# Hashed attention, a Mish feed-forward and eight experts on one core: who decodes the feed-forward weights, when they are converted, and how attention's planner prices transfers

## The chip, the cores and the metric

One core of a Trainium2 chip. The metric is the device time of one execution in microseconds, the median of several runs. Engines are named as in the profile: PE is TensorE's matmul, PEld its weight load, DVE is VectorE, ACT is ScalarE, POOL is GpSimd, SP is the engine that issues the DMA transfers.

## The reference

```
attention:  B,H,S,D = 2,8,768,64;  bits = (q @ proj > 0), six per query and per key
            mask = equal buckets;  attn = softmax(where(mask, q k^T / 8, -1e9));  x = attn @ v
            -> x of 1536 tokens x 512
feed-forward:  h = x @ w_in (512 x 2048, float64 weights);  g = h * tanh(softplus(h));  x = g @ w_out
experts:  logits = x @ w_gate;  P = exp(logits - max), 8 rounds of row and column scaling
          out = sum over 8 experts of P[:, e] * (relu(x @ w1[e]) @ w2[e])      (512 x 1024 x 512 each)
```

The feed-forward weights arrive as 64-bit floats; everything else is float32.

## The kernel before

Three parts follow each other in one instruction stream: attention, the feed-forward, the experts. Every large product is done with operands split into a rounded high part and a low remainder (fp32r), three matmuls per tile: high x high, high x low, low x high.

**Feed-forward.** The hidden width 2048 is cut into 16 chunks of 128; a chunk's weights (its slice of both matrices) are one [128, 1024] array of 64-bit numbers. A step is one chunk for one block of 512 tokens, 48 steps in all: chunks go in groups of 2, 2, 4, 4 and 4, and for each group the three token blocks follow. In step n TensorE does `up(n)` (lines 790 to 801, 12 matmuls: lines 798 and 799 read the weight's high part, line 800 its low part) and `down(n - 3)` (lines 813 to 826, 12 matmuls into four accumulators). In between, `act(n)` (lines 803 to 811) applies Mish and a rounding on ACT and a subtraction on DVE (line 810). At the end of a group the four accumulators are evacuated: the first group by ACT (line 831), the others by DVE (line 833).

**Decoding.** A chunk comes in two halves, each loaded by one 512 KB transfer (line 131) into one of three stage buffers. `decode` turns a half into float32 in eight parts: parts 0 and 1 scale the high and low words on ACT (lines 148 and 150); part 2 clamps (152), part 3 shifts (154), part 4 merges the sign (156), part 5 masks the exponent (160), all on DVE; part 6 multiplies the low word by the power of two, on POOL (162); part 7 adds high and low on DVE or POOL (164) and, in the feed-forward, issues the load of the half three places on. Then `convert_hi` (line 176, ACT) rounds a whole chunk into its place in a ring of eight, and `convert_lo` (line 182, POOL) subtracts to get the low part.

**The order in the feed-forward** is written out by the loop at lines 1059 to 1080. Each engine takes its instructions in that order. A half's parts 0 to 3 come right after the step's `up`, parts 4 to 6 at the end of the step (key d + 0.5), part 7 at the end of the next (d + 1.4). Lines 1042 to 1057 lay the halves out, one every 1.15 steps from step 0, and put the two conversions of a chunk at the end of step t (`at(t, ...)`), t at least two after the step of its second half. Functions registered for n - 1.5 run at the very beginning of step n, before `up(n)`. Chunks 0 and 1 are decoded inside attention.

**Attention.** 16 heads, two units of 384 queries each. Its order is made by a planner when the kernel is built (lines 484 to 751): every piece of work is a task with an engine, a cost, a due time (plus an offset per kind from `OFF`) and the tasks it waits for. The planner takes, per engine, the task with the least "earliest start + DELTA x due", and emits it. For transfers (engine "Q", issued by SP) lines 727 to 730 say when the data counts as landed:

```
free[e] = start + (cost or 0.6)
bus = max(free[e] + 0.5, bus) + lag
ends[k] = bus + RECEIPT
```

Transfers in attention are loads of queries and keys (line 264), of values (270), of the 64-bit weights (131), and copies within the chip (335): six moves of 192 KB for each head, four of bits (18 KB) and one row per unit. `DUE0` and `PACE` set when the four half chunks 0 to 3 are decoded beside attention; their part 6 is a task of engine "P", part 7 of "D" or "P". Three more half chunks are loaded ahead for the feed-forward.

**Experts.** 64 units, lines 1085 to 1284, products of a seven-multiplication scheme (line 1119) and the second product (1186). Nothing in it is touched.

Of the kernel before, what the change touches and what calls it, by code (L numbers as in the profile page):

```python
# [16 lines left out]
P = 128  # L17
# [20 lines left out]
NS = 4  # L38
# [13 lines left out]
COLD = 7.5  # L52
FILL = 256
AHEAD = (1, 2)
OFF = {'weight_lo': 11.0, 'add': -10.2, 'weight_load': -52.8, 'norm6': 87.2, 'prep_hi': 3.9, 'norm_move': -73.0, 'load_qk': -0.2, 'norm0': -29.7, 'load_v': -23.9, 'decode': -0.3, 'bits_mm': 4.8, 'norm1': -110.3, 'norm5': -85.1, 'st_exp': -3.3, 'norm7': 55.1, 'rows_cp': -157.2, 'av_mm': -0.1, 'rows_move': -39.6, 'rows_mm': 3.5, 'norm4': -106.6, 'norm3': 12.6, 'sum_mm': -2.3, 'bits_cmp': -16.6, 'av_one': 12.2, 'weight_hi': 293.4, 's_max': 6.6, 'st_mm': 2.5, 'prep_move': -6.4, 'prep_lo': -4.7, 'bits_move': -9.7, 's_mm': 2.4}
DELTA = 0.0374
RECEIPT = 1.6
DIRECT = 4
DUE0 = 52
PACE = 38  # L60
NX = 1
NATT = 2
FG = 4
# [4 lines left out]
Q = 32  # L68


def f32(t):
    return t[:].bitcast(F32)
# [3 lines left out]
def lsh_attention_moe_kernel(  # L76
# [13 lines left out]
    nc = tc.nc  # L90
# [21 lines left out]
    sgn = [dec_p.tile([P, 512], I32, name=f"sgn{i}") for i in range(2)]  # L112
# [31 lines left out]
    def decode(i, j, part, e="P"):  # L144
        t = staged[i, j]
        lw, hw = t[:, :, 0], t[:, :, 1]
        if part == 0:
            nc.scalar.activation(f32(hw), f32(hw), AF.Copy, scale=SCALE64)
        elif part == 1:
            nc.scalar.activation(f32(lw), lw.bitcast(U32), AF.Copy, scale=2.0 ** -52)  # L150
        elif part == 2:
            nc.vector.tensor_scalar(out=f32(hw), in0=f32(hw), scalar1=HIGH64, scalar2=-HIGH64, op0=ALU.min, op1=ALU.max)
        elif part == 3:
            nc.vector.tensor_scalar(out=sgn[j], in0=hw, scalar1=3, scalar2=None, op0=ALU.logical_shift_left)
        elif part == 4:
            nc.vector.scalar_tensor_tensor(
                out=hw, in0=hw, scalar=-0x80000000, in1=sgn[j], op0=ALU.bitwise_and, op1=ALU.bitwise_or
            )
        elif part == 5:
            nc.vector.tensor_scalar(out=sgn[j], in0=hw, scalar1=-0x800000, scalar2=None, op0=ALU.bitwise_and)  # L160
        elif part == 6:
            nc.gpsimd.tensor_mul(f32(lw), f32(lw), f32(sgn[j]))  # L162
        else:
            (nc.gpsimd if e == "P" else nc.vector).tensor_add(
                dec[i % NDEC][:, j * 512:(j + 1) * 512], f32(hw), f32(lw)
            )
            staged.pop((i, j))
            if auto[0]:
                load_next()
# [18 lines left out]
    def attention():  # L188
        with ExitStack() as a:
# [294 lines left out]
            tasks, ends = {}, {}  # L484

            def task(engines, due, f, *args, after=(), cost=None, lag=0.01, ring=None, frees=None):
                due += OFF.get(f.__name__ + (str(args[1]) if f is norm else ""), 0)
                tasks[f.__name__, *args] = (engines, cost, due, f, args, list(dict.fromkeys(after)), lag, ring, frees)
# [8 lines left out]
                    bits_cmp=0.47, clear=0.7, clear_start=0.85, proj_parts=0.7, gate_parts=0.45,  # L497
# [8 lines left out]
            SEEN = {"E": 0.28, "A": 0.05, "D": 0.05, "P": 0.06}  # L506
            HELD = 0.13
            PICK = (prep_lo, add, norm, decode)
            MOVE = dict(lag=0.87)
            nm = lambda f, *args: (f.__name__, *args)  # L510

            def st_done(u):
                return [nm(st_mm, u, c) for c in range(NKC)] if u >= 0 else []
# [21 lines left out]
            for i in range(NS):  # L535
                for n, kind in enumerate(("sq", "bk", "one")):
                    e = "D" if (kind, i) in FAST else "P"
                    task(e, -8.5 + 3 * i + n / 4, clear, kind, i, after=[nm(clear, "bk", i)] * (n == 2) + [nm(hold)] * (i > 0))

            for h in range(NH):  # L540
                due = 6 * (uses(h)[0] - 3)
                old = uses(h - NS)[1] if h >= NS else -1
                shared = [h for h in range(NH) if h not in (1, 2, *AHEAD)]
                hin = shared[shared.index(h) - NRAW] if h in shared and shared.index(h) >= NRAW else None
                single = [x for x in range(NH) if x not in AHEAD]
                prior = single[single.index(h) - 1] if h and h not in AHEAD else None
                moved = [nm(prep_move, prior, j) for j in range(6)] if prior is not None else []
                task("Q", due - 24 if h else -99, load_qk, h, lag=1.75 if h else -0.35, cost=0.6 if h else 1.2,
                     after=[nm(bits_mm, hin)] + [nm(prep_lo, hin, i) for i in range(2)] if hin is not None else [])
                his = [nm(prep_hi, h, i) for i in range(len(halves(h)))]  # L550
                los = [nm(prep_lo, h, i) for i in range(2)]
                for i in range(len(halves(h))):
                    task("A", due - 14.0 if h else -50, prep_hi, h, i, cost=None if h else 0.45,
                         after=[nm(load_qk, h), *moved])
                for i in range(2):
                    task("PD" if h else "D", due - 14.0 + 1 if h else -50, prep_lo, h, i, after=[his[i if h == 0 else 0], *moved] + [los[0]] * i)
                task("E", due - 10.0 if h else -50, bits_mm, h, cost=None if h else 1.1, after=[nm(load_qk, h), nm(proj_parts)] + [nm(bits_move, h - 2, x) for x in range(4) if h > 2], ring="r" if h else None, frees=nm(bits_cmp, h))
                if h:
                    task("D", due - 9.0, bits_cmp, h, after=[nm(bits_mm, h)] + [nm(bits_move, h - 2, x) for x in range(4) if h > 2])
                else:  # L560
                    for i, j in ((0, 0), (0, 1), (1, 1), (1, 0)):
                        task("D", due - 9.0 + i + 18 * (i > j), bits_cmp, 0, i, j, cost=0.6, after=[nm(bits_mm, 0), nm(load_const, 1), nm(clear, ("sq", "bk")[j], 0)])
                for j in range(6):
                    engine, kw = ("A", {}) if h < 3 and j < 2 else ("Q", MOVE)
                    task(engine, due - 5.0 + 0.1 * j, prep_move, h, j, after=(his if j < 4 else los) + st_done(old), **kw)
                for x in range(4 if h else 0):
                    task("Q", due - 5.0 + 0.5 + x / 8, bits_move, h, x, lag=0.3, cost=0.7,
                         after=[nm(bits_cmp, h), nm(clear, "sq", h % NS), nm(clear, "bk", h % NS)] + st_done(old))

                freed = [av_done(u, NKC // AVG - 1) for x in (h // 2 * 2 - 4, h // 2 * 2 - 3) for u in uses(x)] if h > 3 else []  # L570
                task("Q", 24 * (h // 2) - 20.0, load_v, h, after=freed + [nm(prep_move, 0, j) for j in range(2, 6)] * (h < 2) + [nm(prep_move, 1, j) for j in range(6)] * (1 < h < 4), lag=1.4)
# [3 lines left out]
            for u in range(NU):  # L575
# [9 lines left out]
                ready = [nm(rows_cp, u)]  # L585
                if not direct:
                    ready = [nm(rows_move, u)]
                    task("Q", due + 6.5, rows_move, u, after=[nm(rows_cp, u)] + st_done(u - 2 * NS), lag=0.01)
                ready += [nm(prep_move, h, j) for j in range(6)] + [nm(clear, "one", h % NS)]
                for c in range(NKC):  # L590
                    i = 6 * u + c
# [117 lines left out]
            while count < len(tasks):  # L709
# [16 lines left out]
                    keep_warm(int(max(0.0, real - free[e] - 0.25) / (0.21 if real < COLD else 0.12)))  # L726
                if e == "Q":
                    free[e] = start + (cost or 0.6)
                    bus = max(free[e] + 0.5, bus) + lag
                    ends[k] = bus + RECEIPT  # L730
                else:
                    if cost is None:
                        cost = COST[e][f.__name__]
                    end = real + cost
                    if e == "P" or e == "D" and shares(k):
                        held[e] = end - (0.05 if e == "D" else 0.0)
                    free[e] = end - OVER[e]
                    ends[k] = end + SEEN[e]
# [180 lines left out]
    def at(n, f, *args):  # L919
        side.setdefault(n, []).append(lambda: f(*args))  # L920
# [109 lines left out]
    free = {}  # L1030
# [11 lines left out]
    for i in range(RING_A, N64):  # L1042
        need = free[i - RING] + 1 if i >= RING else 0
        if NATT <= i:
            nd = max(nd, free_dec.get(i - NDEC, 0))
            for j in range(2):
                d = int(nd)
                for part, lag in enumerate((0, 0, 0, 0, 0.5, 0.5, 0.5, 1.4)):
                    early.setdefault(d + lag, []).append((i, j, part, "D"))
                nd += 1.15  # L1050
            need = max(need, d + 2)
        nxt = max(nxt, need)
        t = nxt
        at(t, convert_hi)
        at(t, convert_lo)
        free_dec[i] = nxt + 1
        nxt += 1

# [275 lines left out]
```

## Time and profile before

| | |
|---|---|
| median of 3 runs | 1506.09 us (1505.69 to 1508.87) |
| profiled execution | 1504.85 us, span 1503.1 us, mean granted clock 0.995 |
| PE busy | 1478.4 us, 98% of the span |
| DVE, ACT, POOL busy | 872.1, 638.3 and 910.0 us |
| chain that ended last | PE 94%, DVE 3%, all others 1% or less |
| HBM read | 93.41 MB, 64 GB/s over the span |

Busy times are sums over the whole span; the three parts have different limits, so what matters is read from stretches of it. The chain is followed back from the last instruction to whatever released each one. A wait of an engine is named by the line that waited and the line that released it. PEclk is the share of TensorE's full clock that was granted, as a mean over the stretch.

### The profile page before, as it was taken

How to read it: one execution, taken by the hardware profiler on the slowest of the kernel's cores; microseconds unless marked ns; L12 is line 12 of the kernel's file. 1: busy time of each engine (PE TensorE's matmuls, PEld its weight loads, DVE VectorE, ACT ScalarE, POOL GpSimd, SP SyncE). 2: the span in 40 equal slices, each digit the busy share in tenths (PEclk: the TensorE clock that was granted, in tenths of full speed). 3: DMA queues.
4: the chain of work that ended last, by engine and by line, in shares of the span. 5: the costliest groups of instructions: out<-in, count | busy, mean ns of one | idle time of the engine just before them, and what ended most of it. 6: DMA issues, size and time to landing. Idle time of an engine off the chain costs nothing.

```text
span 1503.1 us, 20188 instructions
## 1 busy us (share of the span) xinstructions
PE 1478.4 (98%) x7452; PEld 1260.5 (84%) x7452; DVE 872.1 (58%) x1406; ACT 638.3 (42%) x1161; POOL 910.0 (61%) x762
## 2 busy tenths in 40 slices
PE   9999999989999999999999999999999999999998
PEld 6666667768887899989899998989989899998987
DVE  7878868858725566665445477653534535344353
ACT  5655666534434343434334333343433334333331
POOL 7778874324322776666666666666666666666660
PEclk9999999999999999999999999999999999999999
DMA  7655512212200122222122222232222122222211
GB/s 190 175 150 156 153 36 98 71 56 84 84 1 15 47 80 70 71 70 71 60 67 70 71 70 71 65 104 70 71 70 70 65 64 69 71 71 71 69 44 42
DMA packets 66490, 116.70 MB, mean 78 GB/s; under 512 B 18276, under 2 KB 20440, under 8 KB 66392
## 3 DMA queue, kind: packets, MB, share of 16 engines
q1 hardware_dynamic: 66392, 115.43, 25.3%
q8 instruction: 58, 0.95, 0.3%
q14 instruction: 40, 0.33, 0.1%
HBM read 93.41 MB, written 3.15 MB: 64 GB/s over the span
## 4 chain that ended last, share of the span: by engine, by line
PE 94%; DVE 3%; DMA 1%; ACT 1%; issue 1%; POOL 1%; SPq 0%; DVEq 0%; POOLq 0%; ACTq 0%
PE y L1186 35%; PE u L1119 31%; PE y L823 7%; PE pav L442 4%; PE h L800 3%; PE h L798 2%; PE h L799 2%; PE pst L414 2%; PE ps L379 2%; PE pst L415 2%; PE psum L452 1%; PE pbits L353 1%; POOL w L182 0%; DMA sb<-hi 0%; DVE mx L384 0%
## 5 line engine op out<-in xcount | busy, mean ns | idle before, releaser
L1127 ACT ACTIVATE gh<-c 128x384 fp32r<-128x384 f32 x256 | 134.6, 526 | 174.2 <-DVE c L1139 172.1
L1139 DVE TENSOR_TENSOR u<-u,p 128x384 f32<-128x384 f32 x64 | 35.7, 558 | 283.8 <-PE u L1119 283.8
L1132 DVE SCALAR_TENSOR_TENSOR gl<-c,gh 128x384 fp32r<-128x384 f32 x256 | 196.0, 829 | 0.0
L1186 PE MATMUL y<-ww,gh 128*128 128x512 f32 x768 | 186.6, 391 | 0.0
L1186 PE MATMUL y<-w,gh 128*128 128x512 f32 x768 | 186.0, 391 | 0.0
L1186 PEld LDWEIGHTS y<-w,gh 128*128 128x128 f32 x768 | 143.7, 188 | 28.9
L1186 PEld LDWEIGHTS y<-ww,gh 128*128 128x128 f32 x768 | 143.7, 188 | 28.8
L1003 POOL TENSOR_TENSOR w<-stage,w 128x1024 fp32r<-128x1024 f32 x32 | 76.5, 2390 | 89.1 <-ACT w L999 89.1
L1003 POOL TENSOR_TENSOR ww<-stage,ww 128x1024 fp32r<-128x1024 f32 x32 | 76.5, 2390 | 81.7 <-ACT ww L999 81.7
L162 POOL TENSOR_TENSOR stage<-stage,sgn 128x512 f32<-128x512 f32 x32 | 42.1, 1317 | 116.2 <-DVE sgn L160 91.6
L823 PE MATMUL y<-gh,w 128*128 128x512 f32 x336 | 110.0, 390 | 0.0
L999 ACT CAST ww<-stage 128x1024 fp32r<-128x1024 f32 x32 | 33.6, 1049 | 157.5 <-PE y L1186 157.5
L979 POOL TENSOR_TENSOR wa<-stage,wa 128x512 fp32r<-128x512 f32 x32 | 45.5, 1423 | 89.2 <-ACT wa L974 80.1
L999 ACT CAST w<-stage 128x1024 fp32r<-128x1024 f32 x32 | 33.6, 1049 | 154.5 <-PE y L1186 154.5
L1186 PE MATMUL y<-ww,gl 128*128 128x512 f32 x384 | 98.2, 389 | 0.0
L1186 PE MATMUL y<-w,gl 128*128 128x512 f32 x384 | 97.7, 389 | 0.2 <-DVE gl L1132 0.2
L979 POOL TENSOR_TENSOR wx<-stage,wx 128x512 fp32r<-128x512 f32 x32 | 45.3, 1417 | 80.7 <-ACT wx L974 80.7
L384 DVE TENSOR_REDUCE mx<-ps 128x1 f32<-128x768 f32 x96 | 88.0, 949 | 9.9 <-PE ps L379 8.5
L420 ACT ACTIVATE p<-pst 128x384 f32<-128x384 f32 x162 | 71.4, 490 | 51.3 <-PE pst L415 44.2
L1119 PE MATMUL u<-tw,w 128*128 128x384 f32 x480 | 91.7, 336 | 0.0
L1119 PE MATMUL u<-tw,ws 128*128 128x384 f32 x480 | 91.6, 336 | 0.0
L810 DVE TENSOR_TENSOR gl<-t,gh 128x512 fp32r<-128x512 f32 x48 | 48.6, 1012 | 64.9 <-ACT gh L809 62.5
(206 smaller groups left out, 3706.9 us busy)
## 6 DMA issues: line engine op xcount, KB each, us to landing
stage<-in_w_dram SPq DMA_DIRECT2D x160, 512.0 KB
raw<-in_qk_dram SPq DMA_DIRECT2D x13, 384.0 KB
sb<-hi SPq DMA_DIRECT2D x20, 192.0 KB
vt<-in_v_dram SPq DMA_DIRECT2D x16, 192.0 KB
out_dram<-acc SPq DMA_DIRECT2D x11, 256.0 KB
wx<-hi SPq DMA_DIRECT2D x14, 192.0 KB
zq<-hi SPq DMA_DIRECT2D x10, 192.0 KB
ak<-hi SPq DMA_DIRECT2D x10, 192.0 KB
```

The lines of the kernel that those rows point to most:

```text
L384: nc.vector.tensor_reduce(out=mx_t[u % 2][:, t:t + 1], in_=s_t.pop((u, t))[:, :, :HALF], axis=AX.XY, op=ALU.max, negate=True)
L420: nc.scalar.activation(p_t[u, c][:, :HALF], st_t.pop((u, c))[:, :HALF], AF.Exp, scale=0.125)
L442: nc.tensor.matmul(av_t[n][64 * e:64 * e + 64, :WIDE], vt[head(u) // 2 % 2][:, c, e, :], p_t[u, c][:, :WIDE], start=(c == 0), stop=(c == N ...
L810: nc.vector.tensor_sub(lo, a, f32(hi))
L823: nc.tensor.matmul(yps[j], x, y, start=(head and m == 0), stop=(tail and m == 2))
L979: nc.gpsimd.tensor_sub(a[:, 1, 0:512], t[:, 0, :], f32(a)[:, 0, 0:512])
L999: nc.scalar.copy(wbuf[u % 2]["w"][:, 0, :], staged["u", u, 1].rearrange("p c n -> p (c n)"))
L1003: nc.gpsimd.tensor_sub(y[:, 1, :], t, f32(y)[:, 0, :])
L1119: nc.tensor.matmul(bank[x], weight(u, a, m, kc), moving(u, b, mm, kc), start=(first and n == 0), stop=(n == 5), skip_group_check=not first)
L1127: nc.scalar.activation(hi, src, AF.Relu)
L1132: nc.vector.scalar_tensor_tensor(out=lo, in0=src, scalar=0.0, in1=f32(hid_u[u, c][0]), op0=ALU.max, op1=ALU.subtract)
L1186: nc.tensor.matmul(y_t[t], (hi, hi, lo)[m][:, t % 3 * P:(t % 3 + 1) * P], y, start=(k == 0 and first), stop=(k == NF // 2 - 1 and last),)
```

## The change

In the feed-forward, part 6 of a decoding is issued on VectorE when `decode` is called with "D" (as the feed-forward does; attention's planner passes "P" for this part). The two conversions of a chunk are registered at t - 1.5, so that they are issued at the beginning of step t instead of its end. Halves are laid out every 1.05 steps. In attention the landing of a transfer is counted from its issue, 1.3 us plus its lag plus 0.5 us, with some lags and costs altered; the offsets, their weight DELTA and the due times of the decoding are new.

```diff
-OFF = {'weight_lo': 11.0, 'add': -10.2, 'weight_load': -52.8, ... 'decode': -0.3, ... 'rows_cp': -157.2, ... 'weight_hi': 293.4, ...}
-DELTA = 0.0374
-RECEIPT = 1.6
+OFF = {'weight_lo': 14.5, 'add': -1.4, 'weight_load': -42.5, ... 'decode': 19.7, ... 'rows_cp': -105.2, ... 'weight_hi': 260.3, ...}
+DELTA = 0.0236
+LATE = 0.5
...
-DUE0 = 52
-PACE = 38
+DUE0 = 68
+PACE = 37
...
-            nc.gpsimd.tensor_mul(f32(lw), f32(lw), f32(sgn[j]))
+            (nc.gpsimd if e == "P" else nc.vector).tensor_mul(f32(lw), f32(lw), f32(sgn[j]))
...
-            MOVE = dict(lag=0.87)
+            MOVE = dict(lag=0.93)
...
-    task("Q", due - 24 if h else -99, load_qk, h, lag=1.75 if h else -0.35, cost=0.6 if h else 1.2,
+    task("Q", due - 24 if h else -99, load_qk, h, lag=1.75 if h else 1.65, cost=0.6 if h else 1.2,
...
-    task("Q", due - 5.0 + 0.5 + x / 8, bits_move, h, x, lag=0.3, cost=0.7,
+    task("Q", due - 5.0 + 0.5 + x / 8, bits_move, h, x, lag=0.3, cost=0.88,
...
-    task("Q", due + 6.5, rows_move, u, after=[nm(rows_cp, u)] + st_done(u - 2 * NS), lag=0.01)
+    task("Q", due + 6.5, rows_move, u, after=[nm(rows_cp, u)] + st_done(u - 2 * NS), lag=0.01, cost=0.75)
...
-                    bus = max(free[e] + 0.5, bus) + lag
-                    ends[k] = bus + RECEIPT
+                    bus = max(start + 1.3, bus) + lag
+                    ends[k] = bus + LATE
...
-                nd += 1.15
+                nd += 1.05
...
-        at(t, convert_hi)
-        at(t, convert_lo)
+        at(t - 1.5, convert_hi)
+        at(t - 1.5, convert_lo)
```

## Rows read from the trace of the kernel before

**Rows 1.** Busy us (x instructions) of each engine by stretch, then PEclk, DMA share, GB/s.
```profile
0.00:219.66 219.66, 212.48 (x1285) 137.85 (x1285) 170.21 (x278) 129.77 (x302) 175.49 (x196) 0.99 0.57 147
219.66:502.40 282.74, 269.22 (x1172) 220.19 (x1169) 189.59 (x269) 124.06 (x203) 97.78 (x62) 0.98 0.17 56
```
**Rows 2.** Waits of PE, whole span: us in total, times, longest.
```profile
PE h L800 <- POOL w L182: 13.5, 3, 6.7
...
PE ps L379 <- DMA sb<-hi: 2.4, 1, 2.4
```
**Rows 3.** Timeline of ACT, Mish of two steps in turn: start, length, [idle before].
```profile
401.11 0.60 ACT L808 ACTIVATE t<-h 128x512 f32<-128x512 f32 x1 [2.09 <-PE h L800]
...
406.55 0.60 ACT L808 ACTIVATE t<-h 128x512 f32<-128x512 f32 x1 [4.19 <-PE h L800]
```
**Rows 4.** Busy us by stretch, behind the second and third wait.
```profile
295.60:300.00 4.40, 4.40 (x12) 3.46 (x13) 3.87 (x6) 0.59 (x1) 1.30 (x1) 0.61 0.39 119
...
309.60:315.00 5.40, 5.40 (x15) 4.28 (x16) 0.00 (x0) 0.92 (x2) 0.00 (x0) 0.63 0.00 0
```
**Rows 5.** Timeline of PE, the matmuls that ended the second and third wait.
```profile
295.56 0.50 PE L800 MATMUL h<-xh,w 128*128 128x512 f32 x1 [3.38 <-POOL w L182]
...
309.60 0.79 PE L800 MATMUL h<-xh,w 128*128 128x512 f32 x1 [6.70 <-POOL w L182]
```
**Rows 6.** Timeline of POOL: products (L162) and subtractions (L182), chunks 3 and 7.
```profile
249.93 1.30 POOL L162 TENSOR_TENSOR stage<-stage,sgn 128x512 f32<-128x512 f32 x1 [2.79 <-DVE sgn L160]
251.19 2.53 POOL L182 TENSOR_TENSOR w<-dec,w 128x1024 fp32r<-128x1024 f32 x1
...
305.96 1.29 POOL L162 TENSOR_TENSOR stage<-stage,sgn 128x512 f32<-128x512 f32 x1 [6.71 <-DVE sgn L160]
307.21 2.34 POOL L182 TENSOR_TENSOR w<-dec,w 128x1024 fp32r<-128x1024 f32 x1
```
**Rows 7.** Timeline of ACT: the roundings of chunks 3 and 7.
```profile
244.56 1.05 ACT L176 CAST w<-dec 128x1024 fp32r<-128x1024 f32 x1 [0.19 <-DVE dec L164]
...
300.56 1.04 ACT L176 CAST w<-dec 128x1024 fp32r<-128x1024 f32 x1
```
**Rows 8.** Line 154 in the whole span: ns shortest/median/longest, first and last start.
```profile
L154 DVE TENSOR_SCALAR sgn<-stage x32: 372/1449/1468, 38.9 to 401.9; 128x512 int32<-128x512 int32 x32
```
**Rows 9.** Timeline of DVE: first decoding of the feed-forward; chunk 7's last addition.
```profile
224.07 0.42 DVE L152 TENSOR_SCALAR stage<-stage 128x512 f32<-128x512 f32 x1
...
295.98 0.68 DVE L164 TENSOR_TENSOR dec<-stage 128x512 f32<-128x512 f32 x1
```
**Rows 10.** DVE's groups from 224 to 330 us: busy us, mean ns | idle before.
```profile
L156 DVE SCALAR_TENSOR_TENSOR stage<-stage,sgn 128x512 int32<-128x512 int32 x16 | 10.9, 682 | 0.0
...
L833 DVE TENSOR_TENSOR acc<-y,acc 128x512 f32<-128x512 f32 x12 | 7.7, 682 | 0.9 <-PE y L823 0.9
L160 DVE TENSOR_SCALAR sgn<-stage 128x512 int32<-128x512 int32 x16 | 6.8, 428 | 0.6
```
**Rows 11.** Busy us by stretch, ahead of the second wait.
```profile
275.00:290.00 15.00, 15.00 (x68) 12.40 (x67) 14.86 (x21) 7.89 (x13) 5.17 (x3) 1.00 0.22 72
```
**Rows 12.** Busy us by stretch, attention's stall.
```profile
85.00:90.00 5.00, 2.65 (x11) 2.33 (x11) 2.12 (x3) 2.39 (x5) 2.30 (x3) 0.83 0.76 176
90.00:95.00 5.00, 5.00 (x30) 3.00 (x28) 3.76 (x5) 2.65 (x6) 4.23 (x4) 0.82 0.13 32
```
**Rows 13.** Chain of waits, 0 to 260 us: start, us from issue to landing, transfer.
```profile
51.35 2.08 DMA sb<-bit
...
80.34 7.10 DMA sb<-hi
...
234.16 3.52 DMA stage<-in_w_dram
```
**Rows 14.** Timeline of SP: the load ahead of that stall.
```profile
77.62 0.51 SPq L264 DMA_DIRECT2D raw<-in_qk_dram  x1
```
**Rows 15.** Timeline of POOL: chunk 1's low part, two halves.
```profile
211.67 2.52 POOL L182 TENSOR_TENSOR w<-dec,w 128x512 fp32r<-128x512 f32 x2
```

## What the change will do to the time, from these rows

> **What bounds the kernel now.** I read the busy time by stretch first, cut where the program's three parts meet. Attention ends and feed-forward's first product starts at 219.66 us; feed-forward ends at 502.40 [rows 1]. TensorE is busy in nearly all of both, so the question is where it is not. The list of its waits has one large entry in the whole span: the third product of a feed-forward step, line 800, which needs a weight's low part from GpSimd (line 182), 13.5 us in 3 times; the next, 2.4 us, is attention's wait for a transfer [rows 2]. The experts' part behind 502.40 has no such wait and the diff does not touch it: I take its 1000.7 us as unchanged.
>
> Feed-forward without loss: one step (24 matmuls) is 5.44 us, the distance of two Mish rows that wait for TensorE [rows 3], so 0.227 us a matmul. The part holds 1172 matmuls [rows 1], 48 steps of 24 and 20 others: 1172 x 0.227 = 266 us. It takes 282.74; 17 us are lost. The second and third wait are 3.38 and 6.70 us, before the matmuls at 295.56 and 309.60 [rows 5]; 3.4 are left for the first. After the second and the third the clock fell: after 3.38 us idle the stretch to 300 has a mean granted clock of 0.61, after 6.70 us idle the stretch to 315 has 0.63, means between the 1.2 and the 2.4 GHz level. 12 matmuls took 4.40 us instead of 2.72, and 15 took 5.40 instead of 3.40: 1.7 + 2.0 = 3.7 us [rows 4]. 13.5 + 3.7 = 17.2 us is all that feed-forward can give.
>
> **Why line 182 is late.** Not for its input. For chunk 3 ScalarE's rounding (line 176) ended at 245.6 [rows 7], and the subtraction began at 251.19: GpSimd's queue holds the decoding products of later half chunks ahead of it, and the one at 249.93 belongs to chunk 4 [rows 6]. For chunk 7 the rounding was issued late, behind a Mish at the end of its step, and ended at 301.6 [rows 7], though the chunk had been decoded by 296.66 (the addition at 295.98, [rows 9]); then the subtraction stood until 307.21 behind chunk 8's product at 305.96 [rows 6]. In front of that product VectorE's queue decides, which is full: 14.86 of 15.00 us busy from 275 to 290 [rows 11].
>
> **The product on VectorE.** Attention hands in "P" for this step, so only the 28 half chunks of feed-forward move. On GpSimd the product takes 1.30 us [rows 6], and while it runs VectorE's shift (line 154) stands: median 1449 ns, the shortest 372 [rows 8]; unhindered it costs about the 0.43 us of the mask, an operation of the same kind [rows 10]. A half chunk on VectorE is now clamp 0.42 + shift 1.45 + merge 0.68 + mask 0.43 + addition 0.68 = 3.66 us [rows 8 to 10]. After: 0.42 + 0.43 + 0.68 + 0.43 + product + addition 0.68. The product on VectorE is not in the trace; its bounds are 0.43 (a one-input line) and 1.30 (GpSimd's row), and I take 0.68, the addition's row, which has the same two inputs and shape: 3.32 us. So VectorE gets about 0.34 us a half chunk back (between -0.28 and +0.59), and GpSimd's queue holds nothing in feed-forward but subtractions and the later expert work.
>
> Here the Trainium skill speaks against the edit: its page Perfetto Trace Analysis, section Optimizing Scalar/DVE Operations, says that VectorE and GpSimd share a port pair under an exclusive lock, so moving work between the two might not help. The trace shows the lock (1449 against 372 ns), but also that the holder's time differs, 1.30 us against the addition's 0.68. By the row 0.34 us a half chunk is freed, by the rule nothing; what follows from nothing is the first rival below.
>
> **Conversions at the beginning of a step.** The rounding and the subtraction of a chunk are issued before the step's own products and decoding, nearly a step earlier in ScalarE's and GpSimd's queues; no instruction is added. New is what stands behind a late decoding: ScalarE's rounding now waits for the last addition ahead of that step's weight scaling and Mish, and TensorE's second product follows three steps (16 us) after the first, so a lateness of a few us costs nothing there.
>
> **Denser decoding.** A half chunk every 1.05 steps instead of 1.15; by the loop's own arithmetic chunks 2 to 4 keep their steps (3, 5 and 7), chunks 5, 6 and 7 are converted in steps 9, 11 and 13 instead of 10, 12 and 14, and 15 in step 30 instead of 33. VectorE's load a step is then 0.95 x 3.32 + gl 0.68 + four evacuations of 0.68 [rows 10] in four steps + 2.53 x 0.48 for the subtractions that block it [rows 6] = 5.7 us against 5.44: over steps 12 to 28 it falls behind by 16 x 0.3 = 5 us, less than the 16 us above.
>
> **What is late next.** Chunk 7, first used in step 15. With no waits step 15 begins at 219.66 + 3 x 2.72 + 12 x 5.44 = 293.1, and its third matmul at 293.6. VectorE cannot end chunk 7's addition before step 12's evacuation: step 12 begins at 276.8, its two products end at 282.2, then four evacuations, gl and the addition, 4.1 us: 286.3. If VectorE's queue is the bound instead: 12 half chunks x 3.32 + 0.85 of the next + 13 gl and 8 evacuations x 0.68 + five subtractions x 2.53 = 67.6 us from 224.07 [rows 9], 291.7. With rounding 1.05 and subtraction 2.53 the low part is there between 289.9 and 295.3: from 3.7 us early to 1.7 late. Chunks 3 and 6, by the same count, come 3 us or more ahead. I take 0.5 us for what remains. Feed-forward: 17.2 - 0.5 = 16.7 us less, with 13 and 17.2 as ends.
>
> **Attention: a new order.** The planner now lets a transfer land 1.3 + lag + 0.5 us after its issue, before 0.6 (or its cost) + 0.5 + lag + 1.6. For lone transfers this is nearer: 18 KB of bits 2.1 us (before 3.1), the chain shows 2.08; 512 KB of weights 3.45 (before 4.35), the chain shows 3.52 [rows 13]. In a queue it is farther off: from the load at 77.62 [rows 14] through five transfers the new count lands the second move at 84.7, the old one at 85.5; it was issued at 80.34 and took 7.10 us, to 87.4 [rows 13]. That was attention's one stall: 2.35 us, and with the clock at 0.83 and 0.82 another 10 x 0.175 = 1.75 [rows 12], together 4.1 us. The offsets reorder everything, with a smaller weight (0.0236), and the weights' decoding gets later due times. No row prices an order that was not run. From above: TensorE idles 219.66 - 212.48 = 7.2 us in attention [rows 1]; with 1.75 of clock 8.9 us could be gained if nothing were left. From below: two new stalls like that one, 8.2 us lost. I take 1.5 us gained, as the counts are better for single transfers and worse for queued ones, and the one known stall (4.1) may go as another comes.
>
> **Sum.** 16.7 + 1.5 = 18.2 us. The profiled execution took 1504.85 us (span 1503.1): 1486.65. The median of the runs shown lies 1.24 above the profiled one, so the forecast is 1487.9.
>
> **Rivals.**
> First, VectorE is the bound and the moved product frees nothing (the rule above). The first two waits still go, since both subtractions then start right behind their rounding. Chunk 7's addition stays at 296.66, low part at 300.2, 6.6 us after 293.6, and about 2.0 us of clock behind it: 17.2 - 8.6 = 8.6 from feed-forward, 1.5 from attention: 1496.0. For it: VectorE's full rows [rows 11]. Against it: the shift's 1.02 us are given back with certainty, and it needs that the product costs all of them.
> Second, attention's new order stalls: two more transfer stalls of 4.1 us with the old one left, 8.2 us instead of -1.5: 1497.6; one, 1493.5. For it: the new count is more hopeful for queued transfers. Against: the old one was too hopeful there as well and cost one stall in 219 us.
> Third, attention loses its stall and two thirds of its idle time in all, 6 of the 8.9 us instead of 1.5: 1483.4. For it the better lone-transfer prices; against it that the other gaps are short and spread, and that part of them is the start, which any order has.
> Fourth, slower than before: decoding in attention slips. Chunk 1's low part ends at 214.2 now [rows 15] and TensorE needs it in step 1, at 219.66 + 2.72 + 0.45 = 222.8. New due times and offset put it 33 units of some 1.08 us later; carried out in full, 36 us, TensorE waits 27 us, more than the 18.2: about 1515. It decides from a slip of 8.6 us on, and beyond 27 us the kernel is slower. Against it: a due time is a weight (33 x 0.0236 = 0.8 us), not a release, and VectorE is busy for 170 of attention's 220 us [rows 1].
> That the product stays on GpSimd is excluded: feed-forward calls every decoding with "D".
>
> **How the numbers follow.** Forecast 0.65, first rival 0.11, second 0.11, third 0.10, fourth 0.03. Range 1482 to 1496: it takes in the third, one stall of the second and most of the first, and leaves out some 0.17 with the tails. 0.2% (3 us) is what a measurement tells from no change: faster 0.95, the same 0.02 and slower 0.03 (the fourth, in part or in full).
>
> **What would show it.** Feed-forward's stretch falls to about 266 us and its mean clock to 1.00; no wait of line 800 for line 182 above 2 us; line 162 (the product) in attention alone on GpSimd, 28 times on VectorE at 0.6 to 0.7 us; the shift's median near 0.43. Attention ends between 214 and 224. Wrong would be: a wait in step 15 of several us (first rival), TensorE waiting for gl (VectorE too far behind), or attention ending past 224.

## The result, and the profile after

| | median us (lowest to highest) | ratio to before [95%] | profiled execution, us | span, us |
|---|---|---|---|---|
| before | 1505.89 (1504.09 to 1508.87) | | 1504.85 | 1503.1 |
| after | 1489.05 (1488.14 to 1489.23) | 0.9885 [0.9868, 0.9902] | 1488.14 | 1486.1 |

16.8 us less; 18.2 were forecast for the profiled execution, 1487.9 for the median. The stretches of the three parts answer to [rows 1]; the fourth line is the stretch of attention in which the old order stalled [rows 12]:

```profile
0.00:218.56 218.56, 211.14 (x1295) 139.07 (x1295) 169.53 (x269) 130.67 (x302) 181.09 (x204) 1.00 0.57 148
218.56:485.40 266.84, 265.67 (x1172) 217.64 (x1169) 192.81 (x297) 123.55 (x203) 66.02 (x36) 1.00 0.18 60
485.40:1486.10 1000.70, 996.63 (x5002) 902.36 (x5000) 512.50 (x860) 384.66 (x656) 637.00 (x504) 1.00 0.22 68
...
80.00:100.00 20.00, 19.53 (x128) 12.80 (x128) 16.31 (x27) 12.01 (x30) 16.47 (x16) 1.00 0.51 136
```

Feed-forward fell from 282.74 to 266.84 us, attention from 219.7 to 218.6, and the experts stayed at 1000.70. The granted clock is 1.00 in all three. TensorE's waits, which answer to [rows 2], hold no line 800 and no line 182 any more. In their place stands a new one of 1.1 us, for VectorE's evacuations (line 833):

```profile
PE ps L379 <- issue: 2.4, 4, 1.1
PE warm L293 <- DVE xh L287: 1.6, 1, 1.6
PE ps L379 <- DMA sb<-hi: 1.6, 3, 1.0
PE y L823 <- DVE acc L833: 1.1, 2, 1.0
```

The moved product and the shift, each over the whole span (ns shortest/median/longest), which answer to [rows 8]:

```profile
L162 DVE TENSOR_TENSOR stage<-stage,sgn x28: 692/694/696, 226.1 to 374.5; 128x512 f32<-128x512 f32 x28
L162 POOL TENSOR_TENSOR stage<-stage,sgn x4: 1300/1301/1306, 79.8 to 210.6; 128x512 f32<-128x512 f32 x4
...
L154 DVE TENSOR_SCALAR sgn<-stage x32: 418/428/1125, 51.9 to 371.8; 128x512 int32<-128x512 int32 x32
```

The product costs 0.694 us on VectorE (0.68 taken) and 1.30 in attention on GpSimd; the shift's median went from 1449 to 428 ns. Chunk 7, the binding one, in the timelines of VectorE, ScalarE and GpSimd, which answer to [rows 6, 7 and 9]:

```profile
286.54 0.68 DVE L164 TENSOR_TENSOR dec<-stage 128x512 f32<-128x512 f32 x1
...
288.94 2.63 DVE L152 TENSOR_SCALAR stage<-stage 128x512 f32<-128x512 f32 x1
...
287.26 1.05 ACT L176 CAST w<-dec 128x1024 fp32r<-128x1024 f32 x1 [5.74 <-DVE dec L164]
...
288.38 2.90 POOL L182 TENSOR_TENSOR w<-dec,w 128x1024 fp32r<-128x1024 f32 x1 [9.30 <-ACT w L176]
```

Addition, rounding and subtraction now follow each other at once. The low part is there at 291.28; TensorE needs it 73.9 us after attention's end (the prediction's 3 x 2.72 + 12 x 5.44 + 0.45), at 292.5. It is 1.2 us early, where 3.7 early to 1.7 late was forecast; the addition ends at 287.22, inside the 286.3 to 291.7 worked out for it. The clamp of 288.94 shows what the subtraction now holds up: it stands 2.63 us where an unhindered one takes 0.42 [rows 9].

### The profile page after: what moved, and what is told of

Its sections match the earlier page's. It is cut to its first block, busy times and chain, and to the rows that moved or that the text cites. A ratio compares the mean times of both kernels' runs of the same rounds, so it can differ in the third digit from the quotient of the medians.

```text
span 1486.1 us, 20163 instructions
## 1 busy us (share of the span) xinstructions
PE 1473.4 (99%) x7463; PEld 1259.1 (85%) x7463; DVE 874.9 (59%) x1425; ACT 638.9 (43%) x1161; POOL 884.1 (59%) x743
## 4 chain that ended last, share of the span: by engine, by line
PE 95%; DVE 3%; issue 1%; ACT 1%; DMA 0%; DVEq 0%; SPq 0%; ACTq 0%
PE y L1186 35%; PE u L1119 32%; PE y L823 8%; PE pav L442 4%; PE h L798 3%; PE h L799 3%; PE h L800 3%; PE ps L379 2%; PE pst L414 2%; PE pst L415 2%; PE psum L452 1%; DVE stage L152 1%; PE pbits L353 0%; PE lg L851 0%; DMA sb<-hi 0%
## 5 line engine op out<-in xcount | busy, mean ns | idle before, releaser
L182 POOL TENSOR_TENSOR w<-dec,w 128x1024 fp32r<-128x1024 f32 (+1 forms) x16 | 38.6, 2413 | 97.7 <-ACT w L176 97.7
L1186 PEld LDWEIGHTS y<-w,gl 128*128 128x128 f32 x384 | 72.0, 188 | 15.5 <-DVE gl L1132 0.6
```

What stands on the lines that cost most here:

```text
L1186: nc.tensor.matmul(y_t[t], (hi, hi, lo)[m][:, t % 3 * P:(t % 3 + 1) * P], y, start=(k == 0 and first), stop=(k == NF // 2 - 1 and last),)
```

## The experiments

"Feed-forward" is the time in the profiled execution from the first weight load of line 798 to the first one of line 1119 that loads `tw`, which comes 1.1 us behind the experts' very first; by it before has 283.8 us and after 267.9.

| kernel | median us | ratio to before [95%] | feed-forward, us |
|---|---|---|---|
| before + product on VectorE | 1487.09 | 0.9882 [0.9863, 0.9900] | 267.8 |
| before + early conversions | 1491.17 | 0.9906 [0.9888, 0.9924] | 272.8 |
| before + denser halves | 1491.55 | 0.9909 [0.9889, 0.9929] | 272.3 |
| before + all three | 1488.54 | 0.9887 [0.9867, 0.9907] | 267.9 |
| after, all three undone | 1505.33 | 1.0000 [0.9987, 1.0013] | 285.1 |
| after, once more | 1490.50 | 0.9908 [0.9887, 0.9928] | 267.9 |
| after, product on GpSimd | 1497.78 | 0.9951 [0.9934, 0.9968] | 277.2 |
| after, late conversions | 1489.13 | 0.9884 [0.9865, 0.9903] | 267.7 |
| after, halves at 1.15 | 1488.19 | 0.9887 [0.9864, 0.9911] | 267.8 |
| before + chunk 6 early | 1505.35 | 0.9999 [0.9985, 1.0013] | 286.3 |
| before + subtraction on VectorE | 1493.52 | 0.9917 [0.9898, 0.9935] | 273.6 |
| before + product and subtraction on VectorE | 1492.05 | 0.9906 [0.9890, 0.9921] | 272.7 |

**Each feed-forward edit alone.** First the product:

```diff
-            nc.gpsimd.tensor_mul(f32(lw), f32(lw), f32(sgn[j]))
+            (nc.gpsimd if e == "P" else nc.vector).tensor_mul(f32(lw), f32(lw), f32(sgn[j]))
```

> The kernel before with one edit: feed-forward's decoding product on VectorE. Theory A (the subtraction of line 182 is late because it stands in GpSimd's queue behind the products of later half chunks, and these behind VectorE's full queue): with the products gone from that queue the first two waits of line 800 vanish; chunk 7 is still converted at the end of step 14, so a wait of 1 to 4 us stays in step 15; time 1489 to 1493 us. Theory R (VectorE is the bound and the moved product frees nothing): three waits of 10 us or more in sum stay, 1501 us or more.

It gives the whole gain by itself: 1487.09 us, feed-forward 267.8. Of line 800's waits one of 1.6 us is left:

```profile
PE h L800 <- POOL w L182: 1.6, 1, 1.6
```

Where it comes from can be taken apart for chunk 7's low part, which is ready at 309.55 before and at 295.30 here, 14.25 us earlier, with due times that are equal (293.6 and 293.5). From the first decoding to chunk 7's last addition, before (busy us of PE, PEld, DVE, ACT, POOL):

```profile
224.07:296.66 72.59, 65.77 (x289) 53.77 (x288) 62.93 (x86) 42.64 (x71) 28.56 (x17) 1.00 0.24 80
```

and with the product moved, where that addition ends at 289.42:

```profile
288.73 0.69 DVE L164 TENSOR_TENSOR dec<-stage 128x512 f32<-128x512 f32 x1
```

```profile
223.99:289.42 65.43, 65.43 (x290) 54.19 (x290) 60.40 (x98) 41.57 (x70) 13.11 (x5) 1.00 0.28 89
```

In the first stretch TensorE stands for 6.8 us (65.77 of 72.59 busy), the first two waits; in the second it never stands. The addition comes 7.2 us earlier: VectorE is busy 2.5 us less (62.93 to 60.40), though 12 products are added to it, and idle 4.6 us less (9.66 to 5.03). But chunk 7's rounding waits for this addition in neither kernel. It stands at the end of its step, behind a Mish that needs TensorE's product. Before, on ScalarE:

```profile
299.41 0.60 ACT L808 ACTIVATE t<-h 128x512 f32<-128x512 f32 x1 [4.12 <-PE h L800]
```

With the product moved, on ScalarE, GpSimd and VectorE:

```profile
290.66 0.60 ACT L808 ACTIVATE t<-h 128x512 f32<-128x512 f32 x1
...
291.82 1.04 ACT L176 CAST w<-dec 128x1024 fp32r<-128x1024 f32 x1
...
292.94 2.36 POOL L182 TENSOR_TENSOR w<-dec,w 128x1024 fp32r<-128x1024 f32 x1 [8.47 <-ACT w L176]
...
291.92 2.48 DVE L833 TENSOR_TENSOR acc<-y,acc 128x512 f32<-128x512 f32 x4
294.31 1.54 DVE L810 TENSOR_TENSOR gl<-t,gh 128x512 fp32r<-128x512 f32 x1
```

Mish and rounding come 8.7 us earlier (300.56 to 291.82 for the rounding), nearly all of it the first two waits and the clock behind the second (3.4 + 3.4 + 1.7). Rounding's end to subtraction's end is 2.4 us instead of 7.95 ([rows 6, 7]: 301.6 to 309.55): 5.5 us, the queue behind chunk 8's product that the prediction had named. 8.7 + 5.5 = 14.2.

Then the conversions:

```diff
-        at(t, convert_hi)
-        at(t, convert_lo)
+        at(t - 1.5, convert_hi)
+        at(t - 1.5, convert_lo)
```

> The kernel before with the conversions at the beginning of a step and nothing else; the product stays on GpSimd. Theory A: the subtractions of chunks 3 and 6 start right behind their rounding, so the first two waits go; chunk 7 is decoded too late by VectorE and a wait of 5 to 7 us in step 15 stays, with up to 2 us of clock behind it: 1495 to 1499 us. Theory R says the same of this kernel; it would be refuted only together with the product alone, which it expects to be no faster than the kernel before.

And the spacing:

```diff
-                nd += 1.15
+                nd += 1.05
```

> The kernel before with half chunks laid out every 1.05 steps and nothing else. Theory A: the first wait (chunk 3, same steps) stays at 3.4 us; chunks 6 and 7 are converted a step earlier in the queues, but behind the same products, so the second and third shrink and do not all vanish: 5 to 9 us saved with the clock, 1497 to 1502 us. Theory R: VectorE is full already, a denser plan decodes no sooner: within 2 us of the kernel before.

Both gave far more than I expected: 1491.17 and 1491.55. The matmuls of TensorE that waited for line 182, with early conversions:

```profile
296.54 0.51 PE L800 MATMUL h<-xh,w 128*128 128x512 f32 x1 [3.16 <-POOL w L182]
```

and with denser halves:

```profile
251.08 0.50 PE L800 MATMUL h<-xh,w 128*128 128x512 f32 x1 [3.46 <-POOL w L182]
...
297.19 0.50 PE L800 MATMUL h<-xh,w 128*128 128x512 f32 x1 [0.71 <-POOL w L182]
```

Early conversions leave only chunk 7's wait, and less than half of it, beside a new one of 1.5 us for ScalarE's line 809; denser halves leave the first as it was and of the later ones 0.7 us. Alone, the three edits take 16.0, 11.0 and 11.6 us off feed-forward. All three on the old attention take 15.9:

```diff
-            nc.gpsimd.tensor_mul(f32(lw), f32(lw), f32(sgn[j]))
+            (nc.gpsimd if e == "P" else nc.vector).tensor_mul(f32(lw), f32(lw), f32(sgn[j]))
...
-                nd += 1.15
+                nd += 1.05
...
-        at(t, convert_hi)
-        at(t, convert_lo)
+        at(t - 1.5, convert_hi)
+        at(t - 1.5, convert_lo)
```

> All three feed-forward edits with attention's old order. Theory A (attention's new order is worth nothing in the mean: old order ended at 216.9, 217.4, 219.6 and 219.66 us in four traces, new order at 218.3 and 218.56): within 1.5 us of the changed kernel run beside it, and of the product alone (1487.1). Theory N (the new order is worth the 1.1 us that the first two traces showed, or more): slower than the changed kernel by 1 us or more.

They do not add: each of them removes most of the same lateness.

**Each edit undone in the kernel after.** The product:

```diff
-            (nc.gpsimd if e == "P" else nc.vector).tensor_mul(f32(lw), f32(lw), f32(sgn[j]))
+            nc.gpsimd.tensor_mul(f32(lw), f32(lw), f32(sgn[j]))
```

> The changed kernel with the product back on GpSimd (early conversions, dense decoding and attention's new order stay). Theory A (each of the three edits alone takes the subtractions out of the late place, they overlap): one wait of at most 4 us in steps 14 or 15 stays, 1489 to 1494 us. Theory P (the product's place is what counts): at least 8 us of the 17 come back, 1497 us or more.

1497.78: 9.4 us of feed-forward come back, more than the 1489 to 1494 that I held likely. The wait has moved to VectorE's evacuations, first in the list of TensorE's waits:

```profile
PE y L823 <- DVE acc L833: 6.7, 5, 2.5
```

and the clock falls behind it, to 0.94 and 0.91 in two stretches:

```profile
265.00:295.00 30.00, 27.16 (x112) 21.66 (x111) 27.83 (x35) 14.03 (x24) 13.16 (x8) 0.94 0.28 89
295.00:315.00 20.00, 18.14 (x73) 14.49 (x72) 19.16 (x26) 7.99 (x14) 7.54 (x5) 0.91 0.25 79
```

So early conversions and denser halves with the product on GpSimd are worse together (277.2) than either alone (272.8, 272.3). Why VectorE comes late to its evacuations in just this mixture no run separates.

The conversions at the end of the step again:

```diff
-        at(t - 1.5, convert_hi)
-        at(t - 1.5, convert_lo)
+        at(t, convert_hi)
+        at(t, convert_lo)
```

> The changed kernel with the conversions back at the end of their step. Theory T (VectorE and GpSimd are one resource by their lock; the waits are one lateness of that resource, met where a weight or a free accumulator is due, and the product's move is the edit that cuts its work): feed-forward from its first to its last product within 2 us of the changed kernel's 267.9, waits of 2 us at most, 1487 to 1491 us. Theory E (the early issue is what keeps the subtraction in time once decoding is dense): waits of line 800 for line 182 of 4 us or more, 1493 us or more.

And the old spacing:

```diff
-                nd += 1.05
+                nd += 1.15
```

> The changed kernel with a half chunk every 1.15 steps again. Theory T: the work per half chunk is what the product's move made it, the spacing matters little: waits of 3 us at most, 1487 to 1492 us. Theory D (chunk 7 needs the step that the denser layout gives it): a wait of 4 us or more in step 15, 1493 us or more.

1489.13 and 1488.19, feed-forward 267.7 and 267.8: with the product on VectorE neither edit is worth anything that these runs can show.

**Three waits or one lateness?** Chunk 6's conversions alone are made early, which takes away what the second wait waits for:

```diff
-        at(t, convert_hi)
-        at(t, convert_lo)
+        at(t - 1.5 * (i == 6), convert_hi)
+        at(t - 1.5 * (i == 6), convert_lo)
```

> The kernel before with one edit: only chunk 6's two conversions are issued at the beginning of their step (12) instead of its end; chunk 7's, product, spacing and attention as before. Theory O (each wait comes from the queue order at its own step): the second wait (3.4 us) and its 1.7 us of clock go, the first (3.4) and the third (6 to 7 us) stay: 1499 to 1502 us. Theory C (cascade: the third wait is there because the second made step 14's evacuation and with it VectorE's queue late): the third wait falls below 3 us with the second gone, 1491 to 1496 us.

Neither theory had it right. The second wait is gone, and the time did not move: 0.9999 [0.9985, 1.0013]. TensorE's waits:

```profile
PE h L800 <- POOL w L182: 11.4, 2, 8.0
...
PE h L798 <- ACT w L176: 1.5, 1, 1.5
PE y L823 <- DVE acc L833: 1.0, 1, 1.0
```

and chunk 7's subtraction on GpSimd, again behind chunk 8's product:

```profile
307.38 1.29 POOL L162 TENSOR_TENSOR stage<-stage,sgn 128x512 f32<-128x512 f32 x1 [5.46 <-DVE sgn L160]
308.62 2.34 POOL L182 TENSOR_TENSOR w<-dec,w 128x1024 fp32r<-128x1024 f32 x1
```

The last wait grew from 6.7 to 8.0 us and two small ones appeared, because chunk 7's low part is ready at 310.96, no sooner than before (309.55). What TensorE does not wait for at chunk 6 it waits for at chunk 7. Two things blur this run. Its trace lost 2.6 us of clock behind the first wait, where that of before lost none (last section); less these, by estimate, chunk 7 would have been ready some 1 us sooner than before. And the moved rounding of chunk 6 stands on ScalarE until its addition is done, ahead of its step's Mish and of the scaling of later halves:

```profile
286.23 1.05 ACT L176 CAST w<-dec 128x1024 fp32r<-128x1024 f32 x1 [4.54 <-DVE dec L164]
```

So part of chunk 7's lateness may be the edit's own; the run shows that this way of removing the second wait gains nothing, not that every way would. With that reserve, the waits can be read as instalments of one lateness: how long after its due time (attention's end + 73.9) chunk 7's low part is ready.

| kernel | ready | due | late, us | feed-forward over after's, us |
|---|---|---|---|---|
| before | 309.55 | 293.6 | 16.0 | 15.9 |
| before + chunk 6 early | 310.96 | 293.4 | 17.6 | 18.4 |
| before + denser halves | 297.14 | 290.8 | 6.3 | 4.4 |
| before + subtraction on VectorE | 298.10 | 292.0 | 6.1 | 5.7 |
| before + early conversions | 296.49 | 291.3 | 5.2 | 4.9 |
| before + product and subtraction | 296.95 | 291.8 | 5.2 | 4.8 |
| before + product | 295.30 | 293.5 | 1.8 | -0.1 |
| before + all three | 292.19 | 293.4 | -1.2 | 0.0 |
| after | 291.28 | 292.5 | -1.2 | 0 |
| after, product on GpSimd | 296.05 | 291.6 | 4.4 | 9.3 |

The last two columns agree within 2 us in all but the last row, where TensorE loses its time at the evacuations instead. In part that must be so: where TensorE waits at this very product and hardly behind it, it is as late as the low part. The table says where the time is paid, not why the part is late. It is read from one trace of each kernel; that it also holds for other chunks was not tried.

**Who should hold the shared resource?** The subtraction, too, can go to VectorE, alone or with the product:

```diff
-            nc.gpsimd.tensor_sub(dst[:, 1, c], source(i)[:, c], f32(dst[:, 0, c]))
+            (nc.vector if auto[0] else nc.gpsimd).tensor_sub(dst[:, 1, c], source(i)[:, c], f32(dst[:, 0, c]))
```

> The kernel before with one edit: feed-forward's subtraction (line 182) on VectorE, the product stays on GpSimd. Theory T: per chunk the two engines hold the shared resource for 5.3 (VectorE's five lines, two halves) + 2.6 (products) + some 1.3 (the subtraction there, twice a 512-wide one) = 9.2 us, as with the product alone (5.3 + 1.4 + 2.5) and against 10.4 before: 1486 to 1492 us. Theory G (GpSimd's product, which holds VectorE's shift in every half chunk, is the cause by itself): VectorE, now with the subtraction too, is later still: 1500 us or more.

```diff
-            nc.gpsimd.tensor_mul(f32(lw), f32(lw), f32(sgn[j]))
+            (nc.gpsimd if e == "P" else nc.vector).tensor_mul(f32(lw), f32(lw), f32(sgn[j]))
...
-            nc.gpsimd.tensor_sub(dst[:, 1, c], source(i)[:, c], f32(dst[:, 0, c]))
+            (nc.vector if auto[0] else nc.gpsimd).tensor_sub(dst[:, 1, c], source(i)[:, c], f32(dst[:, 0, c]))
```

> The kernel before with product and subtraction of feed-forward on VectorE; spacing, place of the conversions and attention as before. Theory T: 5.3 + 1.4 + 1.3 = 8.0 us a chunk, no line of VectorE is held by GpSimd any more (the clamp, shift and gl rows all below 0.75 us), no wait of TensorE above 0.5 us in feed-forward, 1485 to 1488 us. Rival (a VectorE that does everything falls behind with the evacuations): waits for line 833 of 2 us or more, 1490 us or more.

1493.52 and 1492.05. With the subtraction alone on VectorE the products stay in GpSimd's queue, but no subtraction stands behind them, and of line 800's three waits the last alone is left:

```profile
PE h L800 <- DVE w L182: 5.9, 1, 5.9
```

On VectorE the subtraction takes 1.22 us instead of 2.4 to 2.9, which by a count of VectorE's time alone should, with the product there too, have left no wait at all. Yet with both on VectorE the kernel is 5 us slower than with the product alone, by the medians and by feed-forward (272.7 against 267.8). The two were not run side by side, and the intervals of their ratios just touch (from 0.9890 and to 0.9900); the firmer sign is the wait of 4.9 us for the subtraction itself. ScalarE, VectorE and TensorE with both on VectorE:

```profile
290.10 1.04 ACT L176 CAST w<-dec 128x1024 fp32r<-128x1024 f32 x1
...
290.35 2.47 DVE L833 TENSOR_TENSOR acc<-y,acc 128x512 f32<-128x512 f32 x4
292.74 0.68 DVE L810 TENSOR_TENSOR gl<-t,gh 128x512 fp32r<-128x512 f32 x1
...
295.12 0.69 DVE L162 TENSOR_TENSOR stage<-stage,sgn 128x512 f32<-128x512 f32 x1
295.73 1.22 DVE L182 TENSOR_TENSOR w<-dec,w 128x1024 fp32r<-128x1024 f32 x1
...
297.01 0.64 PE L800 MATMUL h<-xh,w 128*128 128x512 f32 x1 [4.93 <-DVE w L182]
```

The rounding ends at 291.14, but the subtraction begins at 295.73, behind four evacuations and the half chunk's lines in VectorE's queue. With the product alone on VectorE (the rows of that kernel above) it begins on GpSimd 0.08 us after its rounding and runs beside the evacuations, which it does not hold: the four take 2.48 us with it and 2.47 without. Only the line after them, gl, takes 1.54 us instead of 0.68. A queue of its own is worth more than the shorter run.

**Attention's new order alone.** The kernel after with the three feed-forward edits undone:

```diff
-            (nc.gpsimd if e == "P" else nc.vector).tensor_mul(f32(lw), f32(lw), f32(sgn[j]))
+            nc.gpsimd.tensor_mul(f32(lw), f32(lw), f32(sgn[j]))
...
-                nd += 1.05
+                nd += 1.15
...
-        at(t - 1.5, convert_hi)
-        at(t - 1.5, convert_lo)
+        at(t, convert_hi)
+        at(t, convert_lo)
```

> The changed kernel with all three feed-forward edits undone, so attention's new order alone. Theory A: feed-forward's waits and clock loss are as before (17 us), attention ends some 1 us earlier as in the changed kernel: 1503.5 to 1506 us. Rival: the later decoding in attention (chunk 1's low part is there only 1.8 us before its use) or the loads left by it shift feed-forward's decoding too, so that feed-forward's waits differ from 13.5 us by more than 2 us.

The ratio is 1.0000 [0.9987, 1.0013]: nothing that ten runs can show, and no more than 2 us either way. Line 800's waits for line 182 are 12.9 us in it, against 13.5 before. The kernel after was also run once more, unchanged, beside the one with the old attention:

> The changed kernel again, unaltered, as the yardstick for the other kernels of this call on the same chip: 1488 to 1490 us by its four earlier runs.

1490.50 against 1488.54, intervals that overlap. Its profiled execution ended attention at 224.4, with these waits of TensorE

```profile
PE ps L379 <- issue: 2.8, 4, 1.6
PE pbits L353 <- DMA xu<-in_qk_dram: 2.0, 1, 2.0
PE ps L379 <- DMA zq<-hi: 1.7, 1, 1.7
```

and a clock of 0.96 in its first 80 us, where the first trace of the same kernel has 1.00:

```profile
0.00:80.00 80.00, 73.41 (x439) 52.34 (x440) 59.58 (x97) 45.86 (x99) 57.82 (x86) 0.96 0.63 163
```

This execution was the slowest of its four (1494.02; the others 1489.45 to 1490.60). The program and its order are the same; its transfers landed otherwise. In the eight traces with the old order attention ends at 216.9 to 219.7 us (median 218.8), in the six with the new one at 217.7 to 224.4 (median 218.5). The old order's stall at 85 us, its clock of 0.91 in the twenty us around it

```profile
80.00:100.00 20.00, 17.55 (x97) 11.83 (x97) 13.81 (x22) 9.94 (x24) 13.11 (x14) 0.91 0.61 153
```

and the new order's 1.00 there are real, but what they give is lost within this spread. The new landing times without the new offsets, and the reverse, were not tried.

## Why the prediction was right

The prediction fell 1.2 us from the median, and its main term holds: feed-forward -15.9 in the two profiled executions and -17.0 by the medians with the old attention (1505.13 x 0.0113; interval 14.0 to 20.0), for 16.7 forecast.

- **The cause, line 182 behind products, these behind VectorE's full queue.** Shown by the product alone: with the products out of GpSimd's queue the first two waits go, 8.7 us with their clock, and 5.5 us of standing behind chunk 8's product. Taking the subtraction out of that queue instead removes the first two waits as well. That the products come late by VectorE is read from the wait of chunk 8's for line 160 (6.71 us, [rows 6]).
- **The product's price.** 0.694 for 0.68. In a stretch without a subtraction, before and with the product alone moved, VectorE's additions are

```profile
283.25 0.68 DVE L164 TENSOR_TENSOR dec<-stage 128x512 f32<-128x512 f32 x1
...
289.74 0.68 DVE L164 TENSOR_TENSOR dec<-stage 128x512 f32<-128x512 f32 x1
```

```profile
284.94 0.68 DVE L164 TENSOR_TENSOR dec<-stage 128x512 f32<-128x512 f32 x1
...
288.73 0.69 DVE L164 TENSOR_TENSOR dec<-stage 128x512 f32<-128x512 f32 x1
```

  The first two starts are 6.49 us apart; less four evacuations (2.39 from start to next start) and gl (0.60) that is 3.50 us a half chunk. The other two, less gl, give 3.19: 0.31 freed, 0.34 forecast. Over the whole way to chunk 7's last addition it is 0.21 (2.5 us by 12 products), with five subtractions in the stretch of either kernel.
- **The first rival, a move that frees nothing.** Refuted: 18 us from that one edit, and 9.4 us lost without it; chunk 7's addition did not stay at 296.66. The Trainium skill's page Perfetto Trace Analysis, section Optimizing Scalar/DVE Operations, says that moving work between these two engines might not help; here it did: VectorE spends 0.69 us on a product and no longer has its shift held for 1.0 us (1449 to 428 ns), but the larger part of the gain is that no subtraction stands behind a product.
- **What stood wrong in the working.** The three waits were added as if each were its own loss, and the rival was priced by letting two of them go for 8.6 us. As a sum of what TensorE lost this holds; as prices of single waits it does not: taking away the second alone gave nothing. The total was right because the change removes the lateness itself, which did not need the single prices. The expectations for early conversions and for denser halves alone, made with the same prices, lay 4 to 10 us too high.
- **Early conversions and denser halves.** The working counts on both; beside the moved product neither gives anything that can be measured.
- **What remains in feed-forward.** 0.5 us was left open. It is the 1.1 us for evacuations, which the prediction did not name.
- **Attention.** 1.5 us of gain were taken between 8.9 gained and 8.2 lost; the runs show 0 within 2. The second and third rival are refuted as the usual case by the medians (0.9987 to 1.0013). But attention's end at 224.4 in one of the six traces lies past the 224 that the prediction named as a sign of being wrong: a loss of the kind that the second rival describes came in that one execution.
- **The fourth rival, decoding that slips.** It did slip. Chunk 1's low part on GpSimd, which answers to [rows 15]:

```profile
217.38 2.53 POOL L182 TENSOR_TENSOR w<-dec,w 128x512 fp32r<-128x512 f32 x2
```

It ends at 219.9 instead of 214.2, 5.7 us later, and TensorE needs it at 218.56 + 2.72 + 0.45 = 221.7. Of 8.6 us slack 1.8 is left: the mechanism was at work, short of the point from which it costs.

## What to carry to other kernels

Several waits for one kind of producer can be one lateness paid in instalments: find the last deadline in the chain and how late it is met, and price an edit by how much sooner that one is met. Edits that shorten the same lateness overlap; run each alone before adding them. An operation that two engines can do belongs where it holds the shared resource shortest, unless it then stands in a full queue that it could have run beside.

## What the runs showed of the hardware

GpSimd's subtraction holds VectorE's lines that read only SBUF and lets the evacuations, one of whose inputs is in PSUM, pass. In after it falls on the clamp; VectorE's group from 223 to 310 us (busy us, mean ns | idle):

```profile
L152 DVE TENSOR_SCALAR stage<-stage 128x512 f32<-128x512 f32 x17 | 22.6, 1331 | 0.0
```

The clamp's mean is 1331 ns where the unhindered one is 0.42 us, while the four evacuations that began 1.0 us ahead of a subtraction, with the product alone moved, took 2.48. The Trainium skill's page SBUF — State Buffer, section Who interferes with whom, says that the pair of ports which the two engines share is an exclusive lock, and that a VectorE instruction with at most one SBUF input, outside the two-port modes, does not contend for it; for the evacuations the trace agrees. The clamp has one SBUF input too and is held, which by that sentence needs a two-port mode; no row here shows the mode.

A wait of one length did not always cost clock. Before, 3.38 us at 292 was followed by a granted clock of 0.61, at a price of 1.7 us [rows 4, 5]; the first wait kept 1.00:

```profile
253.77 0.50 PE L800 MATMUL h<-xh,w 128*128 128x512 f32 x1 [3.44 <-POOL w L182]
```

```profile
250.00:255.00 5.00, 1.55 (x7) 1.04 (x6) 3.90 (x5) 2.52 (x5) 3.71 (x2) 1.00 0.28 89
```

With chunk 6 early the same wait, again 3.44 us long, was followed by 0.50, the 1.2 GHz level:

```profile
254.00:258.00 4.00, 4.00 (x10) 3.06 (x10) 1.72 (x4) 0.00 (x0) 1.30 (x1) 0.50 0.40 131
```

The 12 matmuls from 253.59 to 258.87 took 5.28 us instead of 2.72. So a wait of some 3.4 us cost 2.6, 1.7 or 0 us of clock besides, and its price is to be read behind each wait.
